# Attention followed by a mixture of experts: turning the attention output with fp32 PE transposes one pair later, picks and logits in four column tiles, values two pairs ahead, weights in halves

## The chip, the cores and the metric

The kernel runs on one core of one Trainium2 chip. The metric is the device time of one execution in microseconds; before the change it is 444.41 us, the median of three runs (443.82 to 446.16). The profiled execution has a span of 442.7 us.

## The reference, cut to what matters

Block-causal attention (blocks of 64 positions) over 8 batches, 8 heads, 576 positions, head dimension 64. Its output, laid out as 4608 tokens of 512 features, goes through a gate that picks one of eight experts for each token; the token goes through that expert's two matrices and is scaled by the gate's probability.

```python
# q, k, v: (8, 8, 576, 64) fp32; w_gate (512, 8), w1 (8, 512, 1024), w2 (8, 1024, 512)
scores = scale * np.matmul(q, k.transpose(0, 1, 3, 2))
scores = np.where(pos[:, None] // 64 >= pos[None, :] // 64, scores, -1e9)
attn = softmax(scores)                                  # exp(s - max) / sum
x = np.matmul(attn, v).transpose(0, 2, 1, 3).reshape(4608, 512)

logits = x @ w_gate
expert_idx = np.argmax(logits, axis=1)
gate_w = softmax(logits)[np.arange(4608), expert_idx]
# per expert e, for the tokens with expert_idx == e:
y = np.maximum(x @ w1[e], 0.0) @ w2[e]
out = gate_w[:, None] * y                               # (4608, 512) fp32
```

## The kernel before

The first stage goes through 32 pairs of heads, four pairs to a batch (HP is 4, PAIRS is 32). A pair p has these parts on the engines. PE, ACT (ScalarE) and POOL (GpSimd) run in the order in which the program has them; the order on DVE (VectorE) is set by a scheduler.

- `load`, `load_v`: q and k, and v, from DRAM by SyncE's DMA queue.
- `cast`: POOL makes fp16 of q and k in `h16`.
- `trans`: PE turns q and k (fp16 transposes), DVE copies them to `qkT`.
- `scores`: PE, then exp on ACT into `pt` (and `p4` for the last 64 keys), then small memsets on POOL for the block mask.
- `sums`: DVE adds the blocks of `pt` over keys into `acc`, three additions.
- `attend`: PE makes O^T (features of two heads on the partitions, positions along the row) in fp32 in the PSUM tiles o0 and o1; ACT copies it to `oT`.
- `denominators`: PE sums `acc` over partitions by matmuls with `picks`, 32 columns wide; ACT copies the result to `den`.
- `finish`: PE multiplies each 128 positions of `oT` by `wgi`, an identity with 16 columns of gate weights beside it, which turns the block and gives the unscaled logits; DVE takes reciprocals and multiplies.

```python
oTs = [op.tile([128, 640], F32, name=f"oT{i}") for i in range(2)]
dens = [op.tile([128, 128], F32, name=f"den{i}") for i in range(2)]
acc = op.tile([128, 2, 512], F32)
vts = [op.tile([128, 5, 2, 64], F32, name=f"v{i}") for i in range(2)]
# PSUM: s_ps two slots for scores, o_ps o0 and o1, t_ps two slots named "tp"

def trans(p, n):
    if n == 0:
        st["qkT", p] = c16.tile([128, 2, 576], F16, name="qkT")
    qkT = st["qkT", p]
    ps = t_ps.tile([128, 640], F16, name="tp")
    for c in range(5):
        nc.tensor.transpose(ps[:, c * 128:c * 128 + 128],
                            h16[:, n, c].rearrange("p h d -> p (h d)"), ident16)      # L219
    nc.vector.tensor_copy(qkT[:, n, 0:512]..., ps[:, 0:512]...)                       # L221
    nc.vector.tensor_copy(qkT[:, n, 512:576], ps[:, 512:576])                         # L223

def attend(p, cs, half):
    ...
            nc.tensor.matmul(out=o[h * 64:h * 64 + 64, q0 - lo:hi - lo],
                             lhsT=vt[:, c, h, :], rhs=src, ...)                       # L278
    if cs[-1] == last:
        nc.scalar.copy(oTs[p % 2][:, lo:hi], st.pop(("o", p, half)))                  # L282

def denominators(p):
    pt, p4 = st["pt", p]
    ps = t_ps.tile([128, 128], F32, name="tp")
    # GROUP = (0, 1, 0, 1, 0): blocks 0, 2, 4 and the last 64 keys go to one column
    # tile of a head, blocks 1 and 3 to the other
    ...
                t = 32 * (2 * h + g)
                nc.tensor.matmul(out=ps[t:t + 32, 0:w], lhsT=picks[:, i, :],
                                 rhs=src, start=(n == 0), ...)                        # L300
    nc.scalar.copy(dens[p % 2], ps)                                                   # L303

def finish(p, part):
    ...
    ids = ((0, 1, 2), (3, 4))[part]
    ps = t_ps.tile([128, 512], F32, name="tp")
    if part == 0:
        nc.tensor.matmul(out=ps[:, 432:442], lhsT=den, rhs=sel..., ...)               # L320
    for m, i in enumerate(ids):
        nc.tensor.matmul(out=ps[:, m * 144:m * 144 + 144],
                         lhsT=oT[:, i * 128:i * 128 + 128], rhs=wgi[:, hp, :], ...)   # L324
    ...
    nc.vector.reciprocal(rec..., ps[:, 432:442])                                      # L330
    # for both parts: x16 = rows * rec (L337), lgp = logits * rec (L342)
```

After its fourth pair, `choose` finds each token's expert and `route` its row in a table sorted by expert (some 25 small DVE operations, and matmuls of a triangle of ones on PE); `scatter` writes the rows to DRAM by indirect DMA from POOL, and `load_weights` brings the expert weights as fp16 into `wall` in sixteen parts. The loop is:

```python
for p in range(PAIRS):
    load_v(p + 1); load(p + 3); cast(p + 2)
    sums(p)
    scores(p + 1, 0); scores(p + 1, 1)
    # a scatter of the batch before
    attend(p, (0, 1), 0); attend(p, (0, 1), 1); attend(p, (2, 3, 4), 1)
    trans(p + 2, 0); trans(p + 2, 1)
    scores(p + 1, 2); scores(p + 1, 3)
    # a second scatter; load_weights in 16 of the pairs
    # p % 4 == 0: route(the batch before)
    denominators(p)
    finish(p, 1); finish(p, 0)
    # p % 4 == 3: choose(this batch)
```

The second stage goes through 38 pages of 128 sorted rows: load a page, turn it (PE, DVE copy, L668), multiply by w1 (L680), relu on ACT, turn it, multiply by w2 (L702), scale on ACT (L705), scatter to the output (L706). The last batch is routed while the first pages run.

Of the kernel before, what the change touches and what calls it, by code (L numbers as in the profile page):

```python
# [22 lines left out]
def kernel(  # L23
# [32 lines left out]
    picks = consts.tile([128, 5, 32], F32)  # L56
    wgi = consts.tile([128, HP, 144], F32)

    GROUP = (0, 1, 0, 1, 0)
    sel = consts.tile([128, 5, 2], F32)  # L60
# [9 lines left out]
    place_i = consts.tile([128, NP], I32)  # L70
# [11 lines left out]
    def gate_weights():  # L82
        for hp in range(HP):
            for h in range(2):
                nc.sync.dma_start(
                    out=wgi[h * 64:h * 64 + 64, hp, 128 + h * E:128 + h * E + E],
                    in_=moe_w_gate[hp * 128 + h * 64:hp * 128 + h * 64 + 64, :])

    def constants():
        nc.gpsimd.memset(fill, 0)  # L90
        nc.gpsimd.iota(fill[:, 257:258], pattern=[[0, 1]], base=NO_TOKEN,
                       channel_multiplier=0)

        nc.gpsimd.memset(picks, 0.0)
        for i in range(5):
            nc.gpsimd.memset(picks[:, i, i:i + 1], 1.0)

        nc.gpsimd.memset(wgi, 0.0)
        for hp in range(HP):
            nc.gpsimd.tensor_copy(wgi[:, hp, 0:128], ident32)  # L100
        for i in range(5):
            for h in range(2):
                r = 32 * (2 * h + GROUP[i]) + i
                nc.gpsimd.tensor_copy(sel[:, i, h:h + 1], ident32[:, r:r + 1])

    def route_constants():
# [3 lines left out]
        pref_i = place_i[:, 0:5 * E].rearrange("p (j e) -> p j e", e=E)  # L110
# [22 lines left out]
    def load_weights(n):  # L133
        e, part = n // 2, n % 2
        if part == 0:
            nc.gpsimd.dma_start(
                out=wall[:, e, 0:8, :].rearrange("p (a b) f -> p a (b f)", a=2),
                in_=moe_w1[e].rearrange("(p a b) f -> p a (b f)", a=2, b=2))
        else:
            nc.gpsimd.dma_start(  # L140
                out=wall[:, e, 8:16, :].rearrange("p (a b) f -> p a (b f)", a=2),
                in_=moe_w2[e].rearrange("(p a b) d -> p a (b d)", a=2, b=4))

    with tc.tile_pool(name="ld", bufs=2) as ld, \
# [3 lines left out]
         tc.tile_pool(name="rp", bufs=2) as rp, \  # L148
         tc.tile_pool(name="s_ps", bufs=2, space=bass.MemoryType.PSUM) as s_ps, \
# [6 lines left out]
        dens = [op.tile([128, 128], F32, name=f"den{i}") for i in range(2)]  # L156

        acc = op.tile([128, 2, 512], F32)
# [5 lines left out]
        vts = [op.tile([128, 5, 2, 64], F32, name=f"v{i}") for i in range(2)]  # L164
        p4s = [op.tile([128, 2, 64], F32, name=f"pf{i}") for i in range(2)]

        def borders():
            for i in range(2):
                nc.gpsimd.memset(vts[i][0:64, 4], 0.0)
                nc.gpsimd.memset(p4s[i][0:64], 0.0)  # L170
            nc.gpsimd.memset(acc[:, :, 448:512], 1.0)
            for t in oTs:
                nc.gpsimd.memset(t[:, 576:640], 0.0)
            for t in ohs:
                nc.gpsimd.memset(t, 0.0)
# [19 lines left out]
        def load_v(p):  # L195
            b, h0 = p // HP, 2 * (p % HP)
            vt = vts[p % 2]
# [15 lines left out]
        def trans(p, n):  # L213
            if n == 0:
                st["qkT", p] = c16.tile([128, 2, 576], F16, name="qkT")
            qkT = st["qkT", p]
            ps = t_ps.tile([128, 640], F16, name="tp")
            for c in range(5):
                nc.tensor.transpose(ps[:, c * 128:c * 128 + 128],  # L219
                                    h16[:, n, c].rearrange("p h d -> p (h d)"), ident16)  # L220
            nc.vector.tensor_copy(qkT[:, n, 0:512].rearrange("d (p c) -> d p c", c=4),  # L221
                                  ps[:, 0:512].rearrange("d (c p) -> d p c", c=4))
            nc.vector.tensor_copy(qkT[:, n, 512:576], ps[:, 512:576])  # L223
# [31 lines left out]
        def sums(p):  # L255
            pt = st["pt", p][0]
            nc.vector.tensor_tensor(out=acc[:, :, 0:448], in0=pt[:, :, 128:576],  # L257
                                    in1=pt[:, :, 576:1024], op=ALU.add)
# [5 lines left out]
        def attend(p, cs, half):  # L264

            pt, p4 = st["pt", p]
            vt = vts[p % 2]
# [16 lines left out]
        def denominators(p):  # L284
            pt, p4 = st["pt", p]
            ps = t_ps.tile([128, 128], F32, name="tp")
            todo = [[], []]
            for i in range(5):
                todo[GROUP[i]].append((i, 128))
            todo[GROUP[4]].append((4, 64))  # L290
            for n in range(max(map(len, todo))):
                for h in range(2):
                    for g in range(2):
                        if n >= len(todo[g]):
                            continue
                        i, w = todo[g][n]
                        src = pt[:, h, 0:128] if i == 0 else \
                            acc[:, h, i * 128 - 128:i * 128] if w == 128 else p4[:, h, :]
                        t = 32 * (2 * h + g)
                        nc.tensor.matmul(out=ps[t:t + 32, 0:w], lhsT=picks[:, i, :],  # L300
                                         rhs=src, start=(n == 0),
                                         stop=(n == len(todo[g]) - 1), skip_group_check=True)
            nc.scalar.copy(dens[p % 2], ps)  # L303

        def finish(p, part):

            b, hp = p // HP, p % HP
            oT, den = oTs[p % 2], dens[p % 2]
            if part == 1:
                if hp == 0:  # L310
                    st["x16", b] = xp.tile([128, 5, ROW], I32, name="x16")
                    nc.gpsimd.iota(st["x16", b][:, :, 257], pattern=[[128, 5]],
                                   base=b * S, channel_multiplier=1)
                    st["lg", b] = op.tile([128, 5, H, E], F32, name="lgp")
                st["rec", p] = rp.tile([128, 5, 2], F32, name="rec")
            rec = st["rec", p]
            ids = ((0, 1, 2), (3, 4))[part]
            ps = t_ps.tile([128, 512], F32, name="tp")
            if part == 0:
                nc.tensor.matmul(out=ps[:, 432:442], lhsT=den,  # L320
                                 rhs=sel.rearrange("p i h -> p (i h)"), start=True, stop=True,
                                 skip_group_check=True)
            for m, i in enumerate(ids):
                nc.tensor.matmul(out=ps[:, m * 144:m * 144 + 144],  # L324
                                 lhsT=oT[:, i * 128:i * 128 + 128], rhs=wgi[:, hp, :],
                                 start=True, stop=True, skip_group_check=True)
            st["fin", p, part] = ps
            if part == 1:
                return
            nc.vector.reciprocal(rec.rearrange("p i h -> p (i h)"), ps[:, 432:442])  # L330
            for part, ids in enumerate(((0, 1, 2), (3, 4))):
                n = len(ids)
                ps = st.pop(("fin", p, part))
# [19 lines left out]
        def wide(name):  # L353
            return rp.tile([128, 5, E], F32, name=name)
# [359 lines left out]
        def step(T, n):  # L714
            if T < n:
                m1(T)
# [76 lines left out]
```

## Time and profile before

| engine | busy us of 442.7 | share |
|---|---|---|
| PE | 395.4 | 89% |
| PE weight load | 260.9 | 59% |
| DVE | 253.9 | 57% |
| ACT | 202.3 | 46% |
| POOL | 201.2 | 45% |

The page gives busy time by engine, the same in 40 slices of the span, DMA queues, the chain of work that ended last, and the costliest groups of instructions by line. A share is an average over both stages: the DMA slices, for instance, are at 6 to 9 tenths up to 266 us and at 2 to 3 after. DMA moved 67.58 MB in 80860 packets. So the views below are asked for stretches of single pairs.

### The profile page before, as it was taken

The page shows a single profiled execution, that of the slowest core. Times are in us where ns is not written, and L with a number is a line of the kernel's source. Part 1 is how long each engine was busy: PE and PEld are TensorE (multiplying, and loading weights), DVE is VectorE, ACT ScalarE, POOL GpSimd, SP SyncE. Part 2 cuts the span into 40 slices and gives each one's busy share as a digit, 9 for nine tenths or more (in the row PEclk, how much of TensorE's full clock was granted, in tenths as well). Part 3 has the DMA queues.
Part 4 walks back from the last instruction along what each step waited for, and adds up shares of the span by engine and source line. Part 5 has one row for each costly group of instructions (what it writes and reads, how often), then busy time and mean ns, then how long its engine had stood idle before and what let it go on. Part 6 is the DMA issues. An engine that isn't in the chain of part 4 may idle for free.

```text
span 442.7 us, 11281 instructions
## 1 busy us (share of the span) xinstructions
PE 395.4 (89%) x3870; PEld 260.9 (59%) x3870; DVE 253.9 (57%) x763; ACT 202.3 (46%) x309; POOL 201.2 (45%) x398
## 2 busy tenths in 40 slices
PE   3799899899899799899898896999999999999980
PEld 2466667667676576676766674555555555555540
DVE  3557987977977877977978955422322323323210
ACT  3445555555555355455555441444444434434430
POOL 3854556467375467476484664621221221222230
PEclk9989999999999899999999999999999999999995
DMA  6755969979979878979899569233322322322220
GB/s 182 218 143 143 192 140 229 199 168 233 216 151 239 207 209 184 214 205 200 210 206 217 114 128 210 101 120 98 108 72 97 97 85 96 106 87 76 101 82 24
DMA packets 80860, 67.58 MB, mean 153 GB/s; under 512 B 51919, under 2 KB 75215, under 8 KB 78752
## 3 DMA queue, kind: packets, MB, share of 16 engines
q1 hardware_dynamic: 72448, 34.89, 30.4%
q0 software_dynamic: 7520, 31.31, 30.0%
q8 instruction: 36, 0.59, 0.6%
q10 hardware_dynamic: 832, 0.59, 0.4%
q14 instruction: 24, 0.20, 0.1%
HBM read 67.56 MB, written 17.23 MB: 192 GB/s over the span
## 4 chain that ended last, share of the span: by engine, by line
issue 31%; POOL 22%; DVE 19%; DMA 12%; SPq 2%; PE 1%; ACT 1%; POOLq 1%; DVEq 0%; ACTq 0%
POOL xsorted L451 8%; POOL out_dram L706 7%; DMA qk<-in_k_dram 4%; DMA out_dram<-y,xs 4%; POOL qk L209 3%; DVE acc L257 3%; DVE acc L259 3%; DVE qkT L221 2%; POOL pt L253 2%; DVE x L337 2%; DMA xs<-xsorted 1%; DMA tl<-in_q_dram 1%; DVE acc L261 1%; POOL qk L211 1%; SPq L655 1%
## 5 line engine op out<-in xcount | busy, mean ns | idle before, releaser
L251 ACT ACTIVATE pt<-s 128x1024 f32<-128x1024 f32 x96 | 94.7, 1023 | 81.2 <-PE s L248 30.9
L278 PE MATMUL o<-pt,v 128*64 128x320 f32 (+3 forms) x768 | 92.0, 388 | 0.0
L706 POOL DMA_INDIRECT out_dram<-y,xs x38 | 37.4, 985 | 109.2 <-ACT y L705 108.6
L680 PE MATMUL s<-wall,xsT 128*128 x304 | 71.8, 379 | 3.4 <-DVE lg L364 2.2
L668 DVE COPY xsT<-o 128x512 f16<-128x512 f16 x38 | 16.1, 424 | 99.6 <-PE o L665 99.5
L278 PEld LDWEIGHTS o<-pt,v 128*64 128x64 f32 x768 | 52.1, 139 | 35.7 <-issue 7.4
L702 PE MATMUL tp<-wall,hT 128*128 x304 | 71.6, 379 | 0.0
L221 DVE COPY qkT<-tp 128x512 f16<-128x512 f16 x64 | 43.8, 684 | 32.5 <-PE tp L219 32.5
L253 POOL MEMSET pt<- 64x128 f32 x128 | 23.2, 200 | 82.1 <-ACT pt L251 67.8
L685 ACT ACTIVATE h<-s 128x1024 f16<-128x1024 f32 x38 | 38.9, 1024 | 46.3 <-PE s L680 46.3
L324 PE MATMUL tp<-wgi,oT 128*128 128x144 f32 x320 | 56.8, 312 | 1.7 <-DMA wgi<-in_moe_w_gate_dram 1.7
L451 POOL DMA_INDIRECT xsorted<-x,slot x40 | 48.7, 1218 | 19.3 <-DMA xs<-xsorted 7.5
L209 POOL CAST qk<-qk 128x512 f16<-128x512 f32 x62 | 49.7, 824 | 15.8 <-DMA qk<-in_k_dram 10.4
L680 PEld LDWEIGHTS <-xsT 128*128 128x128 f16 x304 | 29.7, 98 | 38.7 <-DVE xsT L668 2.5
L705 ACT ACTIVATE y<-tp,xs 128x512 f32<-128x512 f32 x38 | 26.2, 689 | 53.5 <-PE tp L702 53.5
L324 PEld LDWEIGHTS tp<-wgi,oT 128*128 128x128 f32 x320 | 44.4, 196 | 4.8 <-issue 2.0
L702 PEld LDWEIGHTS <-hT 128*128 128x128 f16 x304 | 28.4, 98 | 27.1
L257 DVE TENSOR_TENSOR acc<-pt 128x896 f32<-128x896 f32 x32 | 34.8, 1089 | 11.4 <-POOL pt L253 10.0
L282 ACT COPY oT<-o 128x256 f32<-128x256 f32 x64 | 25.7, 402 | 31.7 <-PE o L278 31.7
L248 PE MATMUL s<-qkT 64*128 64x512 f16 (+4 forms) x320 | 33.5, 306 | 2.9 <-DVE qkT L221 2.2
L219 PE MATMUL tp<-ident,qk 128*128 128x128 f16 x320 | 25.2, 225 | 7.8 <-POOL ident L54 5.3
L337 DVE TENSOR_TENSOR x<-tp,rec 128x384 f16<-128x384 f32 x64 | 30.8, 481 | 0.2
(148 smaller groups left out, 481.4 us busy)
## 6 DMA issues: line engine op xcount, KB each, us to landing
wall<-in_moe_w_dram POOLq DMA_DIRECT2D x16, 1024.0 KB, 9.3
qk<-in_q_dram SPq DMA_DIRECT2D x32, 256.0 KB, 4.0
v<-in_v_dram SPq DMA_DIRECT2D x64, 128.0 KB, 4.9
qk<-in_k_dram SPq DMA_DIRECT2D x30, 256.0 KB, 3.4
xs<-xsorted SPq DMA_DIRECT2D x43, 129.0 KB, 2.0
xsorted<-fill SPq DMA_DIRECT2D x1, 1419.0 KB
tl<-in_q_dram SPq DMA_DIRECT2D x32, 32.0 KB, 4.5
v<-in_v_dram SPq DMA_DIRECT2D x32, 32.0 KB, 8.7
```

The source lines that it names most:

```text
L209: eng.tensor_copy(h16[:, n, 0:4].rearrange("p c h d -> p h c d"), qk[:, n].rearrange("p h (c d) -> p h c d", c=4))
L221: nc.vector.tensor_copy(qkT[:, n, 0:512].rearrange("d (p c) -> d p c", c=4), ps[:, 0:512].rearrange("d (c p) -> d p c", c=4))
L251: nc.scalar.activation(pt[:, :, t * 512:t * 512 + 512], sp, AF.Exp, scale=scale)
L257: nc.vector.tensor_tensor(out=acc[:, :, 0:448], in0=pt[:, :, 128:576], in1=pt[:, :, 576:1024], op=ALU.add)
L278: nc.tensor.matmul(out=o[h * 64:h * 64 + 64, q0 - lo:hi - lo], lhsT=vt[:, c, h, :], rhs=src, start=(c == 0), stop=(c == last), skip_group_ ...
L324: nc.tensor.matmul(out=ps[:, m * 144:m * 144 + 144], lhsT=oT[:, i * 128:i * 128 + 128], rhs=wgi[:, hp, :], start=True, stop=True, skip_gro ...
L337: nc.vector.tensor_tensor(out=x16[:, ids[0]:ids[-1] + 1, hp * 128:hp * 128 + 128].rearrange("p i (h d) -> p i h d", h=2), in0=got[:, :, 0: ...
L451: ins = nc.gpsimd.indirect_dma_start(out=xsorted[:, :], out_offset=bass.IndirectOffsetOnAxis(ap=slot[0:m, j:j + 1], axis=0), in_=x16[0:m, ...
L680: nc.tensor.matmul(out=hp[:, half * 512:half * 512 + 512], lhsT=xT[:, c * 128:c * 128 + 128], rhs=weight(T, 2 * c + half), start=(c == 0), ...
L685: nc.scalar.activation(h, hp, AF.Relu)
L702: nc.tensor.matmul(out=yp, lhsT=hT[:, f * 128:f * 128 + 128], rhs=weight(T, 8 + f), start=(f == 0), stop=(f == 7))
L706: ins = nc.gpsimd.indirect_dma_start(out=out[:, :], out_offset=bass.IndirectOffsetOnAxis(ap=xs[:, 257:258], axis=0), in_=y, in_offset=None ...
```

## The change

It touches the first stage and the joint to the second.

- The block of `oT` is turned by a true PE transpose in fp32 against an identity, not by a matmul with one; the two groups of rows that hold denominators and logits (`dl`) are turned with it. This happens for pair p - 1 in the loop's pass p, so that nothing it reads is fresh. `finish` of the last pair and `choose` of the last batch go to the second stage, behind the first page's product with w1.
- The gate logits are made from `oT` in `denominators`, by matmuls with 32 columns of `wg`. Denominators and logits share one PSUM tile in which the column tile is the block of 128 positions, so that four blocks run in four column tiles. DVE copies the result to `dl` at high priority, and the first sum of the next pair is ordered behind that copy.
- q and k are turned in the PSUM tiles o0 and o1, after the last scores; ACT copies q and k alternately with DVE (one each).
- Values are loaded two pairs ahead into three tiles.
- Weights come in 32 parts of 1 MB of fp32, about one a pair, not in 16 of 2 MB.
- Constants: `picks` and `wg` are smaller and set on DVE; gate weights come in two DMAs, not eight. `route` comes a pair later, and the fills of free rows after the loop.

The diff, cut to its core:

```diff
-            ps = t_ps.tile([128, 640], F16, name="tp")
+            ps = o_ps.tile([128, 640], F16, name=("o1", "o0")[n])
...
-            nc.vector.tensor_copy(qkT[:, n, 0:512]...
-            nc.vector.tensor_copy(qkT[:, n, 512:576], ps[:, 512:576])
+            copy = nc.scalar.copy if n else nc.vector.tensor_copy
+            copy(qkT[:, n, 0:512].rearrange("d (p c) -> d p c", c=4),
+                 ps[:, 0:512].rearrange("d (c p) -> d p c", c=4))
+            copy(qkT[:, n, 512:576], ps[:, 512:576])
...
         def sums(p):
-            nc.vector.tensor_tensor(out=acc[:, :, 0:448], ...
+            ins = nc.vector.tensor_tensor(out=acc[:, :, 0:448], ...
+            if p:
+                tc.add_manual_dep(ins.ins, st["dl"].ins.name, ...NoSync...)
...
         def denominators(p):
-            ps = t_ps.tile([128, 128], F32, name="tp")
-            ... t = 32 * (2 * h + g) ... lhsT=picks[:, i, :] ...
-            nc.scalar.copy(dens[p % 2], ps)
+            ps = t_ps.tile([128, 192], F32, name="tp")
+            def add(t, cols, lhsT, src, start=False):
+                nc.tensor.matmul(out=ps[32 * t:32 * t + 32, cols], lhsT=lhsT, rhs=src, ...)
+            lo, hi = slice(0, 128), slice(128, 192)
+            for h in range(2):
+                for j in range(4):
+                    add(j, lo, picks[:, h, :],
+                        acc[:, h, j * 128 - 128:j * 128] if j else pt[:, h, 0:128], h == 0)
+            for h in range(2):
+                add(h, hi, picks[:, h, :], acc[:, h, 384:448])
+            for h in range(2):
+                add(h, hi, picks[:, h, :], p4[:, h, :])
+            for j in range(4):
+                add(j, lo, wg[:, hp, :], oT[:, j * 128:j * 128 + 128])
+            for t in (2, 3):
+                add(t, hi, wg[:, hp, :], oT[:, 512:576])
+            with tc.high_priority():
+                st["dl"] = nc.vector.tensor_copy(dl[:, 0:192], ps)
...
-        def finish(p, part):
-            ... matmuls with den, sel and wgi ...
+        def finish(p, held=None):
+            ps, ps2 = held or (t_ps.tile([128, 512], F32, name="tp") for _ in range(2))
+            for j in range(4):
+                nc.tensor.transpose(ps[:, j * 128:j * 128 + 128],
+                                    oT[:, j * 128:j * 128 + 128], ident32)
+            for n, src in enumerate((oT[:, 512:640], dl[:, 0:128], dl[:, 128:256])):
+                nc.tensor.transpose(ps2[:, n * 128:n * 128 + 128], src, ident32)
+            nc.vector.reciprocal(rec[:, 0:4, :], by_j[:, :, 0:2])
+            nc.vector.reciprocal(rec[:, 4, :], ps2[:, 256:290:33])
+            ... x16 = rows * rec, lgp = logits * rec, for four blocks and for the last ...
...
-                if nxt:
-                    load_v(p + 1)
+                if more:
+                    load_v(p + 2)
...
-                if more:
-                    trans(p + 2, 0)
-                    trans(p + 2, 1)
                 if nxt:
                     scores(p + 1, 2)
                     scores(p + 1, 3)
-                if p > 2 and (p - 3) * 16 // 29 != (p - 4) * 16 // 29:
-                    load_weights((p - 3) * 16 // 29)
-                if p >= HP and p % HP == 0:
+                if more:
+                    trans(p + 2, 1)
+                    trans(p + 2, 0)
+                if p > HP and p % HP == 1:
                     route(p // HP - 1)
...
                 denominators(p)
-                finish(p, 1)
-                finish(p, 0)
-                if p % HP == HP - 1:
-                    choose(p // HP)
+                if p > 2:
+                    for n in range(((p - 3) * 32 + 28) // 29, ((p - 2) * 32 + 28) // 29):
+                        load_weights(n)
+                if p:
+                    finish(p - 1)
+                if p >= HP and p % HP == 0:
+                    choose(p // HP - 1)
...
         def step(T, n):
             if T < n:
                 m1(T)
+            if T == 0:
+                finish(PAIRS - 1, yps)
+                choose(B - 1)
```

## The prediction

> **What bounds the kernel now.** I read the page's slices first: PE is at 8 or 9 tenths from the third slice to the last but one, at full clock, so the TensorE instruction stream is the first suspect in both stages. The stages meet at about 266 us: attention before, the expert pages after. I then asked the windows view for four consecutive pairs (columns: us; busy us and instructions of PE, PEld, DVE, ACT, POOL; clock; DMA share; GB/s).
>
> ```profile
> 164.63:172.00 7.37, 7.03 (x89) 5.17 (x90) 5.08 (x13) 4.20 (x8) 5.36 (x10) 1.00 0.79 164
> 172.00:179.36 7.36, 7.01 (x86) 5.13 (x86) 6.65 (x18) 4.19 (x8) 3.91 (x7) 1.00 1.01 252
> 179.36:188.00 8.64, 7.45 (x92) 5.43 (x92) 8.52 (x41) 4.33 (x9) 4.85 (x10) 1.00 0.95 192
> 188.00:195.70 7.70, 7.06 (x90) 5.24 (x92) 5.74 (x15) 4.32 (x8) 5.39 (x9) 1.00 0.77 205
> sum 31.07, PE 28.56 PEld 20.96 DVE 25.99 ACT 17.04 POOL 19.52; mean PE 7.14 PEld 5.24 DVE 6.50 ACT 4.26 POOL 4.88
> ```
>
> A plain pair costs 7.37 us with PE busy 7.03 of it: PE-bound. The pair that routes a batch costs 8.64, and there DVE is busy 8.52: DVE-bound, four pairs making 31.07. A warning in the last columns but one: the DMA share is 0.77 to 1.01, mean about 0.88, so the four pairs need some 27 us of all 16 DMA engines whatever PE does.
>
> The timeline of PE inside a plain pair gives the length of each part (difference of starts):
>
> ```profile
> 164.62 0.27 PE L300 MATMUL tp<-pt,picks 128*32 128x128 f32 x1 [0.34 <-DVE qkT L223]
> ...
> 165.51 0.76 PE L324 MATMUL tp<-wgi,oT 128*128 128x144 f32 x4
> 166.11 0.29 PE L320 MATMUL tp<-sel,den 128*128 128x10 f32 x2
> 166.25 0.98 PE L324 MATMUL tp<-wgi,oT 128*128 128x144 f32 x6
> 167.16 0.61 PE L248 MATMUL s<-qkT 64*128 64x512 f16 x6
> 167.70 2.81 PE L278 MATMUL o<-pt,v 128*64 128x256 f32 x24
> ...
> 170.56 0.73 PE L219 MATMUL tp<-ident,qk 128*128 128x128 f16 x10
> 171.22 0.39 PE L248 MATMUL s<-qkT 64*128 64x320 f16 x4
> ```
>
> So: picks 0.89 (164.62 to 165.51), finish 1.65 (to 167.16), scores 0.54, attention times values 2.86, q/k transposes 0.66, last scores about 0.42, and 0.34 idle because picks wait for the PSUM slot that the q/k copy on DVE still reads. The parts sum to 7.36.
>
> From the groups by form I take what one instruction costs. An fp32 matmul appears as two load-and-matmul records; the second number is the mean ns of one record.
>
> ```profile
> L278 PE MATMUL o<-pt,v 128*64 128x320 f32 x384 | 58.0, 434 | 0.0
> L278 PE MATMUL o<-pt,v 128*64 128x192 f32 x128 | 16.4, 326 | 0.0
> L324 PE MATMUL tp<-wgi,oT 128*128 128x144 f32 x320 | 56.8, 312 | 1.7 <-DMA wgi<-in_moe_w_gate_dram 1.7
> L221 DVE COPY qkT<-tp 128x512 f16<-128x512 f16 x64 | 43.8, 684 | 32.5 <-PE tp L219 32.5
> L337 DVE TENSOR_TENSOR x<-tp,rec 128x384 f16<-128x384 f32 x32 | 17.6, 550 | 0.2
> ```
>
> A record's length is a fixed latency plus its stream: 434 less 326 ns is 108 ns for 128 columns. An fp32 matmul of 128 columns thus occupies its column tile for two records, 0.213 us. The five finish matmuls of 144 columns (0.24 each), the one over den (0.23, its two weight loads) and two borders make the 1.65.
>
> **What the Trainium skill says.** "TensorE: Matmul & The Clock Gate", section Terms, says that trn2's transpose mode is four times faster for FP32. No fp32 transpose runs in the kernel before, so the trace can't confirm it; this is the largest open size of the prediction. The same page, section LDWEIGHTS, gives a load as columns over 1.2 GHz, 107 ns for 128. The trace agrees for fp32, in a timeline line of the den matmul:
>
> ```profile
> 253.43 0.31 PEld L320 LDWEIGHTS tp<-sel,den 128*128 128x128 f32 x2
> ```
>
> Two loads span 0.31 us at 0.19 each, so they start 0.12 apart. "TensorEngine Tiling (Array Packing)", section Available Configurations, allows four tiles of 128x32; in the trace four picks start within 20 ns of each other, so they do run side by side. Its section Key Properties says a change of tiling mode drains the engine; the trace has about 0.1 us at such borders, and the change has as many of them as before.
>
> **The change part by part.**
>
> Finish on PE. Removed: ten records on wgi and two on den, 1.65 us. Added: seven fp32 transposes of 128x128. With one pass each, the weight load is what paces them: 7 x 0.107 = 0.75, plus 0.1 for the border, 0.85. Gain 0.80 a pair.
>
> Picks. Before, two of four column tiles carried a third and fourth step, so the depth was 128+128+128+64 columns. Now: two steps of 128 on four tiles (0.43), two of 64 on two tiles (0.21), the logits as one step of 128 on four tiles (0.21) and one of 64 (0.11): 0.96, with the border 1.07 against 0.89. Loss 0.18.
>
> PSUM slots. The q/k transposes move from the t_ps ring to the two O tiles, free by then: both halves were copied out by ACT while the last scores ran. The 0.34 wait of picks goes.
>
> Pair on PE: 7.36 - 1.65 - 0.89 - 0.34 + 0.85 + 1.07 = 6.40 us, 0.96 less.
>
> DVE. It loses one q/k copy with its tail (0.68+0.18) to ACT and gains the copy of dl (estimate 0.35 from the 0.19 of a 48-column copy and about 1.05 ns a column) and one more reciprocal (0.2); the products keep their elements. Some 0.3 less. In a plain pair the DVE now does acc, reciprocals, products and two more acc in about 4.1 us (before: 3.7 from the first acc to the last product of a plain pair, 165.57 to 169.26), well before the next picks need acc, 5.3 us after the last ones. In the routing pair some 25 small operations stand before the last acc. Before, the stretch from the rank copy at 180.4 to the next q/k copy at 187.4 took 7.0 us, 3.3 more than a plain pair's 3.7; some 0.6 of that was waiting, so I take 2.7. With 0.35 for dl and 4.1, acc is ready about 7.2 us after the picks, which wait about 1.9. The pair that chooses adds 0.3. Four pairs: 4 x 6.40 + 1.9 + 0.3 = 27.8 against 31.07.
>
> ACT goes from 4.2 to about 5.0 us a pair, POOL is unchanged: both under 6.4.
>
> DMA. Same bytes. Four pairs still need about 27 us of the engines, so at 27.8 they would run at 0.98. The windows view over 20 to 266.6 us has a mean share of 0.82, 202 us of work. I allow 28.3 for four pairs with weights. Against that, half-size weight parts, one per pair, and values two pairs ahead should remove the one large stall, where two weight loads came 15 us apart and the chain shows
>
> ```profile
> 133.59 11.64 DMA qk<-in_k_dram
> ```
>
> which is worth 5 us over two pairs; it lies inside the average of before.
>
> Start and joint. The first pair loses its finish: its successor's scores start at 23.9 us after a 1.7 wait for the gate weights and the finish behind it; now at about 20. Scores of pair 1 to the end of attention: three pairs without weights at 6.5 and 28 at 28.3/4 give 218; the end moves from 266.6 to 238, 28 us earlier. At the joint, page 0 waits for the order of pages, now computed one pair later: about 1 us; but choose of the last batch no longer stands before the first page product (2.2 us of PE idle on it before). The last finish, 0.85, falls into the expert stage, whose page pitch of 4.17 us is untouched. Sum: 444.4 - 28 - 1 + 1 = 416; I add 2 for waits that I don't see: 418.
>
> **The rivals.** (a) An fp32 transpose takes two records like a matmul: 7 x 0.213 + 0.1 = 1.6, no gain in finish; a pair is 7.15, four with a shorter routing wait 29.8, total about 432. For it: every fp32 operation in this trace is doubled. Against: the skill's sentence. I give it a quarter. (b) DMA becomes the bound: at a share near 1 the casts wait for q and k as they did at 133.59, and four pairs take 29 to 30: 424 to 430. For it: the share of 1.01 in one pair; against: the mean of 0.82. (c) DVE becomes the bound: in-order dl copies, sums and products now sit in the loop that frees PSUM for PE (the dl copy must be done before the last three transposes). Its busy time, 25.99 of 31.07 now, would be about 25 of 27.8. If a dl copy regularly stands behind a 1.09 us sum, a pair loses up to 1 us and the gain is nearly gone: 440. The manual order of the first sum after the dl copy speaks against it. (d) The transposes are shorter than the loads suggest and DMA is elastic: 410.
>
> **Range and chances.** Predicted 418 us. The low end, 408, is (d) with nothing lost; the high end, 434, covers (a) and (b). Faster by over 2% means under 435.5: (a) and (b) still satisfy it, only (c) or a mix of (a) and (b) does not. Chances: faster 0.87, within 2% 0.11, slower 0.02.
>
> **What would show it.** Right: plain pairs of about 6.4 us; seven transposes in about 0.85 us with one record each; routing pairs 1.5 to 2.5 longer, released by an acc row of DVE; DMA share in the weighted windows at 0.95 or more; a page pitch still at 4.17. Wrong: 14 transpose records a pair; PE waiting for the dl copy in plain pairs; casts on POOL waiting for q or k in most pairs; a joint longer than before.

## The result and the profile after

The changed kernel takes 419.97 us, the median of four runs (418.52 to 420.52); the kernel before took 445.29 beside it. The ratio is 0.944, with a 95% interval of 0.939 to 0.948. The profiled execution has a span of 418.6 us where before it was 442.7.

The windows view of the changed kernel for four consecutive pairs (two plain ones, the one in which experts are chosen and ranked, the one in which VectorE routes) has the columns that the prediction named:

```profile
175.58:182.07 6.49, 6.49 (x95) 4.51 (x93) 4.91 (x13) 4.53 (x8) 6.05 (x12) 1.00 0.99 168
182.07:188.57 6.50, 6.50 (x95) 4.51 (x93) 5.03 (x12) 4.53 (x9) 5.27 (x11) 1.00 1.09 257
188.57:196.16 7.59, 6.81 (x101) 4.77 (x99) 7.42 (x28) 4.66 (x9) 3.87 (x11) 1.00 1.08 271
196.16:203.66 7.50, 7.10 (x95) 4.64 (x93) 7.10 (x33) 4.53 (x8) 4.80 (x8) 1.00 1.09 263
sum 28.08, PE 26.90 PEld 18.44 DVE 24.45 ACT 18.25 POOL 19.99; mean PE 6.73 PEld 4.61 DVE 6.11 ACT 4.56 POOL 5.00
```

In a plain pair PE is now busy from end to end: 6.50 of 6.50. Four pairs make 28.08 instead of 31.07. The DMA share stands at 0.99 to 1.09, so a share of 1 is no ceiling in this view, and in the plain pairs PE doesn't wait for transfers.

The timeline of PE inside the plain pair from 182.07 (start, length, instruction):

```profile
182.13 2.81 PE L272 MATMUL o<-pt,v 128*64 128x256 f32 x24
...
184.99 0.39 PE L238 MATMUL s<-qkT 64*128 64x320 f16 x4
...
185.34 0.73 PE L208 MATMUL o<-ident,qk 128*128 128x128 f16 x10
186.01 0.30 PE L285 MATMUL tp<-pt,picks 128*32 128x128 f32 x1
...
187.05 0.65 PE L315 MATMUL tp<-ident,oT 128*128 128x128 f32 x4
187.61 0.33 PE L318 MATMUL tp<-ident,oT 128*128 128x128 f32 x1
187.77 0.38 PE L318 MATMUL tp<-ident,dl 128*128 128x128 f32 x2
188.09 0.61 PE L238 MATMUL s<-qkT 64*128 64x512 f16 x6
```

Read by differences of starts: picks with logits 1.04 (186.01 to 187.05), the turn 1.04 (to 188.09). Each fp32 transpose is one record: four on L315, three on L318. Nothing stands idle ahead of the picks.

The gain is not all in the pairs. I divide both spans at the same three points: the end of the attention's last TensorE instruction, the start of page 0's second product, the end of the last page's second product.

```
                                      before    after   difference
start to end of attention             266.73   236.98     -29.75
end of attention to page 0's product   10.91    22.69     +11.78
pages                                 151.97   152.02      +0.05
last product to end of program         13.07     6.88      -6.19
span                                  442.68   418.56     -24.12
```

Two of the four differences were not in the prediction: the joint of the stages gave 11.8 us back, and the end of the program gained 6.2. Of the 11.8, 8.4 lie ahead of page 0's transposes (L659), which follow the attention without a gap before and start 8.2 us after its end now, and 3.4 lie between them and the second product.

At the joint the timeline of PE shows the loss, and the chain of waits shows what page 0 waited for:

```profile
236.60 0.38 PE L318 MATMUL tp<-ident,dl 128*128 128x128 f32 x2
245.19 0.61 PE L659 MATMUL o<-ident,xs 128*128 128x128 f16 x4 [8.22 <-DMA xs<-xsorted]
247.00 3.57 PE L674 MATMUL s<-wall,xsT 128*128 x8 [1.19 <-DMA xsorted<-fill,frows]
...
254.34 1.89 PE L674 MATMUL s<-wall,xsT 128*128 x8 [1.85 <-DVE xsT L662]
```

```profile
233.38 0.97 POOL xsorted L442
234.35 0.59 POOL wall L124
...
235.24 7.08 DMA xsorted<-x,slot
242.69 0.38 SPq L649
```

The last row scatter of batch 6 goes out at 235.24, behind weight parts asked for at 230.36 and 234.35 on the same queue, and lands 7.08 us later; only then does SyncE ask for page 0. PE is idle for 8.22 us. The first products after that take 3.57 us, the next ones 1.89: the windows view has the granted clock at 0.50 from 240 to 252 us.

In the kernel before, the same chain reads:

```profile
260.03 3.62 DMA xsorted<-x,slot
...
264.03 0.37 SPq L655
```

There the scatter went out 6.70 us ahead of the end of the attention (266.73) and page 0 was asked for 2.70 ahead of it; now the scatter goes out 1.74 ahead and page 0 is asked for 5.71 behind.

At the end, the trace has an instruction named drain on GpSimd behind the last output scatter: 8.49 us before (from 433.37), 2.52 after (from 414.83). That is 6.0 of the 6.2 us.

### The profile page after: what moved, and what is told of

Read it like the earlier page. It is cut to its first block, busy times and chain, and to the rows that moved or that the text cites. A ratio compares the mean times of both kernels' runs of the same rounds, so it can differ in the third digit from the quotient of the medians.

```text
span 418.6 us, 11596 instructions
## 1 busy us (share of the span) xinstructions
PE 381.7 (91%) x4094; PEld 238.6 (57%) x4094; DVE 238.1 (57%) x767; ACT 212.4 (51%) x341; POOL 198.5 (47%) x400
## 4 chain that ended last, share of the span: by engine, by line
issue 29%; PE 26%; DVE 14%; DMA 13%; POOL 12%; ACT 3%; SPq 2%; POOLq 1%
PE o L272 11%; POOL out_dram L700 8%; PE tp L285 5%; DMA out_dram<-y,xs 4%; PE s L238 3%; DMA tl<-in_k_dram 2%; PE o L208 2%; DMA wall<-in_moe_w_dram 2%; DVE acc L247 2%; POOL xsorted L442 2%; PE tp L315 2%; DVE x L326 2%; ACT pt L241 2%; DVE acc L253 2%; PE tp L318 2%
## 5 line engine op out<-in xcount | busy, mean ns | idle before, releaser
L674 PE MATMUL s<-wall,xsT 128*128 x304 | 73.5, 385 | 3.1 <-DVE xsT L662 1.8
L272 PEld LDWEIGHTS o<-pt,v 128*64 128x64 f32 x768 | 51.0, 139 | 36.7 <-issue 7.9
L442 POOL DMA_INDIRECT xsorted<-x,slot x40 | 45.4, 1136 | 30.5 <-DVE em_h L506 14.5
L198 POOL CAST qk<-qk 128x512 f16<-128x512 f32 x62 | 45.0, 746 | 15.4 <-DMA qk<-in_q_dram 7.3
L247 DVE TENSOR_TENSOR acc<-pt 128x896 f32<-128x896 f32 x32 | 37.4, 1168 | 2.4 <-POOL pt L243 2.4
L211 DVE COPY qkT<-o 128x512 f16<-128x512 f16 x32 | 22.0, 686 | 24.9 <-PE o L208 24.9
L326 DVE TENSOR_TENSOR x<-tp,rec 128x512 f16<-128x512 f32 x64 | 31.1, 485 | 0.0
L689 DVE COPY hT<-o 128x1024 f16<-128x1024 f16 x38 | 26.2, 691 | 7.3 <-PE o L686 4.8
L285 PE MATMUL tp<-acc,picks 128*32 128x128 f32 (+1 forms) x512 | 27.7, 264 | 2.9 <-DVE acc L255 1.7
L208 PE MATMUL o<-ident,qk 128*128 128x128 f16 x320 | 24.6, 226 | 5.3 <-POOL ident L54 5.2
```

Of the source, the lines that this page charges most:

```text
L198: eng.tensor_copy(h16[:, n, 0:4].rearrange("p c h d -> p h c d"), qk[:, n].rearrange("p h (c d) -> p h c d", c=4))
L247: ins = nc.vector.tensor_tensor(out=acc[:, :, 0:448], in0=pt[:, :, 128:576], in1=pt[:, :, 576:1024], op=ALU.add)
L285: nc.tensor.matmul(out=ps[32 * t:32 * t + 32, cols], lhsT=lhsT, rhs=src, start=start, stop=True, skip_group_check=True)
L326: nc.vector.tensor_tensor(out=x16[:, j:j + n, hp * 128:hp * 128 + 128].rearrange("p i (h d) -> p i h d", h=2), in0=rows.rearrange("p (i h ...
L442: ins = nc.gpsimd.indirect_dma_start(out=xsorted[:, :], out_offset=bass.IndirectOffsetOnAxis(ap=slot[0:m, j:j + 1], axis=0), in_=x16[0:m, ...
L674: nc.tensor.matmul(out=hp[:, half * 512:half * 512 + 512], lhsT=xT[:, c * 128:c * 128 + 128], rhs=weight(T, 2 * c + half), start=(c == 0), ...
```

## The experiments

The changed kernel is the base of all but one. The runs fell on several chips, and that matters here. On the chip of runs 1 to 4, on that of 5 to 8 and on that of 12 the kernel before takes 450 to 452 us; on the chip of 9 to 11 it takes 445, as on that of the result. Run 5 is the changed kernel again, and runs 1 to 8 are read against it. The changed kernel was not run on the chip of runs 1 to 4; the kernel before takes the same there as on that of run 5 (449.88 and 449.93).

**1. Weights in 2 MB loads again.**

```diff
-        e, part, a = n // 4, n // 2 % 2, n % 2        # 32 parts of 1 MB
+        e, part = n // 2, n % 2                       # 16 loads of 2 MB, as before
...
-                    for n in range(((p - 3) * 32 + 28) // 29, ((p - 2) * 32 + 28) // 29):
-                        load_weights(n)
+                if p > 2 and (p - 3) * 16 // 29 != (p - 4) * 16 // 29:
+                    load_weights((p - 3) * 16 // 29)
```

> The changed kernel with the weights in sixteen 2 MB loads again, as before; all else as changed. If the gain is the shorter PE pair, two pairs of prefetch hide the bigger lumps: 420 to 424 us, plain pairs still 6.5. If the gain is the smoother DMA traffic: 430 us or more, with POOL casts that wait for q and k for several us as before.

Measured: 442.09 us (441.45 to 446.19), 9.2 over run 5. The attention ends at 259.53 against 255.37, 4.2 later, and the drain at the end is 8.40 us against 2.67: 5.7 more. The waits view of this run from 60 to 235 us shows the casts of q and k held again:

```profile
POOL qk L202 <- DMA qk<-in_k_dram: 17.7, 6, 4.6
```

(total, times, longest). In run 5 the same wait over the same stretch is 1.0 us, once. PE in turn waits 4.5 us for these casts here, in three times, and not at all in run 5. So smaller parts do let q and k through, as the prediction had it, but more than half of what they bring is at the end of the program.

**2. The turn by fp32 matmuls with the identity instead of transposes.**

```diff
-                nc.tensor.transpose(ps[:, j * 128:j * 128 + 128], oT[:, j * 128:j * 128 + 128],
-                                    ident32)
+                nc.tensor.matmul(out=ps[:, j * 128:j * 128 + 128],
+                                 lhsT=oT[:, j * 128:j * 128 + 128], rhs=ident32, ...)
```

> The seven fp32 transposes of finish are fp32 matmuls with the identity (same output). If finish is on the path of a pair: two records of 0.107 us instead of one of about 0.145, so 0.5 us more in a plain pair (7.0) and 9 to 15 us in all, 429 to 435. If DVE or DMA sets the pair: under 3 us.

Measured: 444.97 us (444.53 to 445.91), 12.1 over run 5. The timeline of PE in one of its plain pairs:

```profile
202.77 1.16 PE L315 MATMUL tp<-ident,oT 128*128 128x128 f32 x8
203.76 0.39 PE L319 MATMUL tp<-ident,oT 128*128 128x128 f32 x2
203.99 0.61 PE L319 MATMUL tp<-ident,dl 128*128 128x128 f32 x4
204.53 0.61 PE L238 MATMUL s<-qkT 64*128 64x512 f16 x6
```

Fourteen records and 1.76 us where the transposes have seven and 1.04; the plain pair is 7.21 instead of 6.49, in run 5 too. The transpose itself, not the later turn, is worth 0.72 us in a pair that PE fills. The pairs that route don't get longer (8.24 on average here, 8.39 in run 5), so the attention ends 8.6 later (263.98 against 255.37); most of the rest is at the joint.

**3. No weights loaded** (GpSimd writes zeros to the weight tiles instead, so the output is zero).

```diff
-        nc.gpsimd.dma_start(out=wall[...], in_=src[:, a, :])
+        nc.gpsimd.memset(wall[...].bitcast(F32), 0.0)
```

> The expert weights are not read: POOL clears the tiles instead, so the output is zero and 33.5 MB less are read in the attention stage. If PE bounds the plain pairs and DVE the choosing and routing pairs: plain pairs stay at 6.5 and four pairs stay at 27.5 to 28.1 us. If the DMA engines bound the four pairs: 26.5 or less.

Measured: 440.44 us in one run. The plain pair of this kernel in the windows view:

```profile
189.58:196.07 6.49, 6.49 (x95) 4.51 (x93) 4.82 (x13) 4.53 (x9) 5.02 (x10) 1.00 0.61 160
```

With a DMA share of 0.61 the pair is 6.49, the same as at 1.09. Transfers don't set the plain pair. Four pairs are 29.4, more than either forecast, because those that route are 8.83 to 8.87 us in five of six cases. They, a drain of 7.1, and 11.3 us for which VectorE is held at pair 31 (of which below) keep the total high.

**4. The last two weight parts behind the last scatter of batch 6.**

```diff
-                if p > 2:
+                if 2 < p < PAIRS - 2:
...
             scatter(B - 2, 4)
+            load_weights(30)
+            load_weights(31)
```

> The last two weight parts are issued behind the last scatter of batch 6, ahead of the fills. If the joint's 8 us of PE idle come from the scatter landing behind the weight parts in one queue (7.1 us from issue to landing): it lands in about 4, page 0 is turned at 240 to 241 instead of 245.2, and the total is 414 to 416. If the landing has its own cause: 419 to 421.

Measured: 434.93 us (431.97 to 435.85) against 432.86 in run 5: no gain. On this chip it could not show one: PE comes to the joint so late, at 257.2, that page 0 is there and it doesn't wait.

**5. The changed kernel again.**

> The changed kernel once more, with nothing altered, as the measure for the others of this call. In the four kernels before, two things came out longer than in the profile of the changed kernel although their edits did not touch them: the pairs that route took 8.2 to 8.8 us instead of 7.3, and the stretch from the exponentials of pair 31 to the end of the attention 20 to 25 us instead of 12.8. Theory C: that belongs to the chip or to the day, not to the edits; then this run too shows routing pairs above 8 us and takes 428 to 436 us. Theory E: it belongs to the edits; then this run repeats 418 to 421 us with routing pairs near 7.3 us.

Measured: 432.86 us (430.35 to 436.36); ratio 0.962 (0.955 to 0.969) to the kernel before on the same chip. So theory C: the longer routing pairs (8.14 to 8.61 us, 8.39 on average, where the result's profile has 7.34) and the longer end of the attention are the chip's. The timeline of VectorE at pair 31, and the chain of waits with SyncE's page loads:

```profile
244.33 0.25 DVE L541 TENSOR_SCALAR on<-place,at 128x33 f16<-128x33 f32 x1
254.06 0.36 DVE L301 COPY dl<-tp 128x192 f32<-128x192 f32 x1 [9.48 <-remote]
```

```profile
248.27 0.38 SPq L649
...
249.70 0.34 SPq L649
...
251.15 0.69 SPq L649
```

PE had delivered picks and logits by 245.1, and no other work stood in VectorE's order. SyncE goes from one page load to the next in 1.43 and 1.45 us (248.27, 249.70, 251.15), and the fourth comes 2.81 later. In the profile of the result the same loads start at 242.69 and follow each other in 0.91, 0.85 and 0.83. Both times GpSimd is issuing the eight row fills one after another; after they end, at 254.0, SyncE's step here is 0.83 too. The span is 12.5 us longer than in the profile of the result: 7.7 up to pair 31, mainly from the routing pairs, and 10.7 from there to the end of the attention, less 6.5 at the joint, where page 0 has now landed before PE asks for it.

**6. The end of the attention rearranged.**

```diff
+                if p == PAIRS - 1:
+                    scatter(B - 2, 4)
...
-            scatter(B - 2, 4)
+            finish(PAIRS - 1)
+            choose(B - 1)
+            load_weights(30)
+            load_weights(31)
             for e in range(E):
...
-            if T == 0:
-                finish(PAIRS - 1, yps)
-                choose(B - 1)
```

> Three edits where the attention meets the pages: pair 31 is turned at the end of the attention instead of after the first page's matmuls, the last scatter of batch 6 goes out one pair earlier, and the last two weight parts behind it. Theory: page 0 waits for that last scatter's landing, and then for VectorE with the products of pair 31. Then the time from the end of the attention to the second product of page 0 falls from 22.7 us to 11 to 15, and the run is 7 to 11 us under the changed kernel on the same chip (about 409 to 413 if that one is 420). Rival: the first page is held by the order of pages or by the fills of rows, not by that scatter; then it gains under 3 us.

Measured: 432.96 us (432.42 to 433.40), the same as run 5. The joint did shrink, from 16.2 to 13.3 us, but the attention ended 2.6 later, under the same row fills. The edit was also imperfect: the order on PE put the turn of pair 31 between page 0's transposes, not ahead of them.

**7. Values one pair ahead again.**

```diff
-                if more:
-                    load_v(p + 2)
+                if nxt:
+                    load_v(p + 1)
```

> Undoes one part: the values are loaded one pair ahead again. Theory: in the changed kernel's plain pairs of 6.5 us a load asked for one pair ahead still lands in time with the weights in 1 MB parts, as it nearly did before; the part is worth at most 0.1 us a pair, so 0 to 4 us over the changed kernel on the same chip. Rival (transfers bound the pairs): a shorter pair leaves too little time for the landing, TensorE waits for the values at the head of the attend, and the run is 10 to 25 us longer.

Measured: 433.45 us (430.04 to 435.67) against 432.86. No difference that these runs can measure, and PE never waits for values in its waits view. This part of the change costs a buffer and brings nothing that shows on this chip.

**8. The kernel before, with only the q/k transposes moved.**

```diff
-            ps = t_ps.tile([128, 640], F16, name="tp")
+            ps = o_ps.tile([128, 640], F16, name=("o1", "o0")[n])
...
-                if more:
-                    trans(p + 2, 0)
-                    trans(p + 2, 1)
                 if nxt:
                     scores(p + 1, 2)
                     scores(p + 1, 3)
+                if more:
+                    trans(p + 2, 1)
+                    trans(p + 2, 0)
```

> The kernel before with one part alone: the transposes of queries and keys behind the last scores, into the two tiles of O instead of the shared small ones. My step said that this takes away the 0.34 us that TensorE waits for a free small tile in each pair: 29 pairs by 0.34 us is 10 us, so 433 to 437 us where the kernel before is 444. Rival: the wait moves to the copies of queries and keys on VectorE ahead of the next scores, and the time stays within 3 us of before.

Measured: 443.56 us, median of four runs that lie from 435.94 to 448.72, where before takes 449.93 on this chip. Three of them, the profiled one too, ran in a slower state; the other, 435.94, lies in the forecast range, but a single run does not size the part. The pair does. Two plain pairs, in the windows view of this run:

```profile
182.82:189.78 6.96, 6.96 (x88) 5.14 (x86) 5.20 (x13) 4.09 (x8) 6.17 (x12) 1.00 0.66 181
222.83:229.85 7.02, 7.02 (x88) 5.19 (x86) 5.32 (x13) 4.19 (x7) 5.24 (x11) 1.00 1.01 267
```

PE is busy without a gap, 6.96 and 7.02 instead of 7.37: 0.35 to 0.41 less, where the step said 0.34.

**9. The copy of denominators and logits on ScalarE.**

```diff
-            with tc.high_priority():
-                st["dl"] = nc.vector.tensor_copy(dl[:, 0:192], ps)
+            nc.scalar.copy(dl[:, 0:192], ps)
```

(with the manual order of the first sum behind that copy taken out)

> The changed kernel with one instruction per pair moved: the 128x192 copy of denominators and logits (dl) goes to ScalarE instead of VectorE. In the second run of the changed kernel VectorE stood idle ahead of that copy until GpSimd had issued its row scatters and fills: 1.46 us in each pair that routes, and 9.5 us at pair 31, although TensorE had long delivered. Theory P: a VectorE copy and GpSimd's issue of an indirect transfer keep each other out; ScalarE is not concerned. Then the pairs that route fall from 8.4 to 7.3 us, the stretch from the exponentials of pair 31 to the end of the attention from 23.5 to 12 or 13, and the run from 433 to 415 to 421 us. Theory D: the landing of a transfer (the scatter, or rows that they read) holds VectorE; the engine that copies makes no difference, and the run stays within 4 us of the changed kernel. ScalarE has 2 us free in a pair of 6.5; plain pairs may grow by up to 0.2.

Measured: 421.06 us (419.41 to 424.56), at the edge of theory P's range. But the kernel before took 445.25 on this chip, and run 11, which leaves the copy on VectorE, took 421.94 on it with routing pairs of 7.7 us and no long wait at pair 31. That wait was not there to cure, so the run does not test P. Run 12 does. In its own right the move is a trade: five of six routing pairs of 6.95 to 7.39 us where run 11 has 7.55 to 7.81, and plain pairs of 6.64 instead of 6.49. This run and run 10 also have one pair in which PE waits 4 to 5 us for a cast whose k is late; whether that comes of the move is not shown.

**10. The same with the edits of run 6.**

> The copy on ScalarE together with the three edits at the end of the attention (pair 31 turned there, the last scatter of batch 6 one pair earlier, the last two weight parts behind it). With theory P both stretches shrink, and the first page no longer waits for VectorE: 5 to 9 us under the run with the copy on ScalarE alone, 408 to 414. Rival: the page's loads are held by the row fills that GpSimd issues one after the other, 1.3 us each; then these edits gain under 3 us again.

Measured: 421.87 us (418.10 to 423.25), no gain over run 9. SyncE asks for page 0 at 237.04, 5.65 us earlier than in the result's profile, and PE gets it no earlier. PE's timeline, and two slices of the windows view:

```profile
236.96 0.38 PE L313 MATMUL tp<-ident,dl 128*128 128x128 f32 x2
245.28 0.51 PE L659 MATMUL o<-ident,xs 128*128 128x128 f16 x3 [7.94 <-DMA xs<-xsorted]
```

```profile
240.00:242.00 2.00, 0.00 (x0) 0.00 (x0) 0.00 (x0) 0.00 (x0) 1.70 (x4) 0.97 1.06 214
242.00:244.00 2.00, 0.00 (x0) 0.00 (x0) 0.00 (x0) 0.00 (x0) 1.60 (x3) 0.50 1.03 248
```

The transfer engines are full. In the trace's packets, 3 of the page loads' 1032-byte packets start before 241 us, 77 between 241 and 243, beside 83 of the 4096-byte packets of the two weight parts asked for at 235.4 and 236.0, and 202 between 243 and 244, when the weights are nearly through. In the result's profile the same slices have shares of 0.31 and 0.23: there the engines were mostly idle while the scatter was awaited. One wait took the place of another, and both end at 245. The run also shows what held the scatter: with no weight part among the last five, page 0 is asked for 2.63 us after the last one is issued (234.41 to 237.04), where the result's profile has 7.45.

**11. Weights in 64 parts of 512 KB.**

```diff
+        for u in range(2):
-        nc.gpsimd.dma_start(out=wall[...], in_=src[:, a, :])
+            nc.gpsimd.dma_start(out=wall[... half u ...], in_=src[:, a, 1024 * u:1024 * u + 1024])
```

> The changed kernel with the weights in 64 parts of 512 KB, each 1 MB part split in two, otherwise the same. Asked is the end of the program: GpSimd's last drain took 8.5 us with 16 weight transfers on its queue, 7.1 with none, and 2.5 to 3.2 with 32. Theory N: more transfers on that queue make the drain shorter; with 64 it takes under 2.6 us. Rival W: what counts is where the queue stands at the end, which wraps around; then the drain takes some other length, over 4 us. The attention may lose up to 4 us to 32 more issues of 0.6 us on GpSimd.

Measured: 421.94 us (420.36 to 423.52). The last drain takes 4.66 us. Theory N falls: with 86, 102, 118 and 150 transfers on GpSimd's queue in all, the drain took 7.1, 8.4 to 8.5, 2.5 to 3.2 and 4.7 us. It changes with the number, but not in one direction. The 4.66 us are what rival W allowed, over 4, which doesn't show that W is the rule; that stays open.

**12. Run 10 with the turn ahead of page 0 and the weight parts behind the fills.**

```diff
-            finish(PAIRS - 1)
-            choose(B - 1)
-            load_weights(30)
-            load_weights(31)
             for e in range(E):
                 fill_rows(e)
+            load_weights(30)
+            load_weights(31)
...
+            finish(PAIRS - 1, yps)
+            choose(B - 1)
             mtx(0)
```

> The run before last with the edits at the end of the attention put right: pair 31 is turned ahead of page 0's transposes (in that run the order on TensorE had it between them, so behind the wait for page 0), and the last two weight parts are asked for behind the eight row fills instead of ahead of them, so that the loads of the first pages have the transfer engines nearly to themselves. The copy of denominators stays on ScalarE. Theory L: with the last scatter out early, SyncE asked for page 0 at 237.0, but it landed only 7.4 us later, beside 1 MB weight parts asked for at 235.4 and 236.0. Then page 0 is now on TensorE 2.5 to 4 us after its load is asked for, from the end of the attention to the second product of page 0 it is 13 to 15 us instead of 19.4, and the run takes 414 to 418 us where the kernel before takes 445 (and, if theory P holds, 414 to 421 on a chip where the kernel before takes 450; 425 or more there speaks against P). Rival: the page loads wait for something else, or the parts now come late for the pages of expert 7; then the gain stays under 2 us.

Measured: 438.21 us (436.51 to 440.23), ratio 0.970 (0.966 to 0.974), on a chip where the kernel before takes 451.95. Theory P falls: with the copy on ScalarE the routing pairs are 8.00 to 8.06 us in five of six cases, not 7.3, and the stretch from pair 31's exponentials to the end of the attention is 29 us. In pair 30 ScalarE starts this copy at 242.48, 3.0 us after PE's last record for it has ended (239.52). PE's timeline at pair 31 shows why the engine that copies makes no difference:

```profile
247.50 0.28 PE L281 MATMUL tp<-acc,picks 128*32 128x128 f32 x1 [0.48 <-issue]
248.24 0.27 PE L281 MATMUL tp<-acc,picks 128*32 128x128 f32 x1 [0.46 <-issue]
248.97 0.28 PE L281 MATMUL tp<-acc,picks 128*32 128x128 f32 x1 [0.46 <-issue]
...
254.62 0.37 PE L281 MATMUL tp<-acc,picks 128*32 128x128 f32 x1 [0.99 <-issue]
256.02 0.67 PE L281 MATMUL tp<-acc,picks 128*32 128x128 f32 x8 [1.03 <-issue]
```

These matmuls wait for nothing that the profile shows; in a plain pair 36 such records take 1.04 us, here eight take 8.5 (247.50 to 256.02). This ends within a microsecond of GpSimd's last issue (255.1). Of theory L one part showed: from the end of the attention to page 0's second product it is 12.9 us, and PE no longer waits long for page 0. But the attention itself, which here includes the turn of pair 31, ended later, so the gain at the joint could not be told from that. On a chip of the other kind this version was not run, and none here beats the changed kernel.

## Why the prediction was right

The attention stage came out as predicted, and for the reason given: a plain pair that PE fills, made shorter by the steps named. That the total, 418 us, lies within 2 of 420 is in part luck. Two unseen terms, +11.8 at the joint and -6.2 at the end of the program, leave +5.6; the attention's 1.75 beyond the 28 expected and the 2 us added for unseen waits cover most of that. By steps:

- **Finish on PE, 0.85 us.** The mechanism was right and the size was not: 1.04. Each is one record, as I had taken from the Trainium skill's sentence that trn2's transpose mode is four times faster for FP32 ("TensorE: Matmul & The Clock Gate", Terms). But they come slower than a load of 0.107 us: the four on L315 take 0.56 from start to start, 0.14 each. The skill's factor of four is not what the kernel gains: against the matmul form of run 2, 1.76 to 1.04, it is 1.7.
- **Picks and logits, 1.07.** Right: 1.04.
- **The wait for a PSUM slot, 0.34.** Right: gone here, and 0.35 to 0.41 when moved alone (run 8).
- **Plain pair, 6.40.** 6.49, by the finish term less small ones. Rival (a) was wrong as a prediction and right as a size: run 2 makes it, and the plain pair is 7.21 where (a) said 7.15.
- **DVE, 1.9 us in the routing pair and 0.3 in the choosing one.** The sum of 2.2 was right (7.59 and 7.50 less 6.49 each: 2.1), the division was not. In the fourth window picks and logits last 2.10 us (200.06 to 202.16 in PE's timeline) instead of 1.04, waiting for acc: 1.06, not 1.9. In the third the rank matmuls stand, 0.3 us with their border, and wait 0.78 for the choice of experts; in the whole run PE waits so for 4.7 us in seven times. With the turn one pair later, choosing stands directly ahead of ranking.
- **DMA, 28.3 for four pairs.** 28.08; but the reason, a bound near a share of 1, was wrong. Run 3 has the same plain pair at a share of 0.61. Rival (b), casts that wait for q and k, does not set the pairs; it shows in single stalls, with 2 MB loads (run 1) and in one pair each of runs 9 and 10. The stall at 133.59, put at 5 us, cost 2.8: the two pairs take 19.23 us between them, their like 16.45.
- **End of the attention at 238.** 236.98.
- **The joint, no change.** This is the step that failed. I looked at the order of pages and at choose, and not at what else page 0 waits for: all row scatters of the first seven batches. In the kernel before, the last of them stands behind the loop too, but outside the part in which GpSimd's order is fixed, and it went out at 260.03, ahead of seven of the row fills. The change routes a pair later, fixes this scatter behind the last pair and gives the same queue a weight part per pair to the very end, so it goes out later against the end of the attention and lands in 7.08 us instead of 3.62. Run 10 shows that the scatter is not the whole of it: with page 0 asked for earlier, its load waits beside the weight parts instead. Whether routing at the old place would have kept the joint short was not tried.
- **The page pitch, 4.17.** Unchanged.
- **The end of the program** was not in the prediction. Runs 1, 3 and 11 show the drain change with what went through GpSimd's queue, and no rule for it.

The gain also depends on the chip: 0.944 on one, 0.962 on another (run 5). The change has GpSimd issue a scatter and eight row fills in a row while pair 31 is still to be finished; before, one fill went out at 253.95 and seven from 261.80 on, most of them beside the pages. On some chips the other engines crawl while GpSimd issues them. The parts are not separate gains either: of the 17.1 us that the change brings on the chip of run 5, undoing the transposes takes 12.1 and undoing the smaller weight parts 9.2. The turn a pair later, the four column tiles and ScalarE's share of the q/k copies were never undone alone.

## What to carry to other kernels

When a stage gets shorter or its parts move by a pair, list everything that its successor waits for, with the queue that each item goes through: transfers that used to end inside the stage can come out at the joint, and taking away the wait that ends last may only uncover the next. Look at the end of the program as well as at the stages, since a change of transfers can move it by microseconds. When experiments land on different chips, run the changed kernel among them, or the chip's effect is read as the edit's.

## What the runs showed of the hardware

- While GpSimd issues indirect transfers back to back (1.29 us apart), other engines on three chips issue slowly: SyncE's page loads go from 0.83 to 1.43 us apart and VectorE stands idle 9.48 us (run 5), PE issues a matmul in 0.7 us or more (run 12). On the chip of the result and that of runs 9 to 11 SyncE's step is 0.83 to 0.97 during the same fills, but for single steps. It is not a matter of VectorE alone (run 12). What is shared stays open.
- This program's last drain on GpSimd took 2.5 to 8.5 us: 7.1 after 86 transfers on its queue, 8.4 to 8.5 after 102, 2.5 to 3.2 after 118, 4.7 after 150.
- After PE's last instruction at the joint the granted clock fell to 0.50 after 2.1 us in the profile of the result and after 4.6 in run 10; eight products of 512 columns took 3.57 us instead of 1.89 in the former.
